# A third home for one chunk's inputs, weights converted by pairs, and attention pieces placed by hand in the first unit

## The chip, the cores and the metric

One Trainium2 chip, one of its cores. The metric is the time of one execution on the device in microseconds (us); lower is better. Engines are named as the profile names them: PE is TensorE (PEld its weight loads), DVE is VectorE, ACT is ScalarE, POOL is GpSimd, SP is SyncE, which here only issues DMAs.

## The reference

```python
# 1: linear attention with decay, B=4, H=8, S=768, D=48
for t in range(S):
    state = alpha[:, :, t, :, None] * state + np.einsum('bhd,bhe->bhde', k[:, :, t], v[:, :, t])
    y[:, :, t] = np.einsum('bhd,bhde->bhe', q[:, :, t], state)
# 2: x = y as [3072 tokens, 384]; squared-ReLU layer, d_ff = 2048
h = np.maximum(x @ w_in, 0.0)
x = h * h @ w_out
# 3: 8 experts, each token to one of them by its sorted gate logits, 384 tokens an expert
logits = x @ w_gate
...
    h = np.maximum(x[mask] @ w1[e], 0.0)
    out[mask] = h @ w2[e]
```

The weights `w_in` and `w_out` come into the kernel as 64-bit floats and are made into 32-bit ones on the chip.

## The kernel before

The tokens are cut into 24 chunks of 128 (six to a batch entry), and three chunks make a unit of 384 tokens: 8 units. Attention (`attn`) is done by chunks, and the squared-ReLU layer by units: for each of 16 blocks `f` of 128 hidden features, `moe_a` multiplies the unit's tokens into a PSUM tile `ph` (line 388, 9 matmuls), `moe_ev` squares the ReLU and splits it into a high and a low part `hl` (for unit 0: three ACT passes at lines 393, 397 and 401, then a DVE subtraction at line 404), and `moe_b`, two steps later, multiplies `hl` by the block of `w_out` (line 416, 9 matmuls). Each product is made of three, with both factors split in two, so that it has nearly the precision of 32 bits.

A step is one value of `g` (unit and block). The first 18 steps, `first_step`, are the first unit and the first two blocks of the second one. They are under a hand-written order: on PE, DVE, ACT and POOL instructions stand as the code emits them, and a queue that waits holds all that is behind it. What stands ahead of the first step is listed in `ORDER`: the letters name pieces of chunks 0 to 3 (`p` and `a` two scans on DVE, `q` the scaled `kt` and `qt`, `s` the scores, `n` a transposed `kn`, `o` the result), `C` and `S` the two parts of a weight conversion, `w` a dummy matmul.

What each step of the first unit holds besides `moe_a`, `moe_ev` and `moe_b`:

- Conversion. Two blocks of weights a step (one of `w_in`, one of `w_out`), each in `narrow`: three integer passes on DVE over 128x384 words (lines 348, 350, 352), from a raw tile `rawi` or `rawo` into `wf` or `wfo`. In the next step, ACT rounds the block into `wbuf` (line 355), and POOL subtracts for the low part (line 356). A raw tile is loaded again as soon as its third pass is over; `rawi` has three homes, `rawo` two.
- The gate columns (`gate_w`): the expert gate is folded into `w_out`, so each block of `w_out` is transposed on PE (line 450), copied by ACT (line 452), multiplied by the gate weights into eight spare columns of `ph` (line 455), and split into `wbuf` by ACT (line 457) and DVE (line 459).
- Attention for the next units: `attend` gives a number of pieces for the step, by `PACE`, and they are emitted behind `moe_b`. Chunks 3 to 6 are done in this way within the 18 steps.

Two PSUM banks hold `ph`. The matmuls at line 388 of step `g` can start only when the last reader of the bank of step `g - 2` is done; that is line 459, which stands behind line 404 on DVE.

The inputs of a chunk (alpha, k, q; 677 KB) go to one of two tiles `akq0`, `akq1`. Chunk 2 therefore waits until chunk 0 has let go of its tile.

## Time and profile before

| What | Value |
|---|---|
| Time, median of 3 runs | 868.7 us (868.61 to 869.08) |
| The profiled execution: its time, and its span | 867.91 us, 865.7 us |
| PE busy | 813.1 us, 94% of the span |
| DVE busy | 498.1 us, 58% |
| ACT, POOL busy | 337.6 us, 366.3 us |
| Mean granted TensorE clock | 0.975 of full speed |

The span runs from the first to the last instruction on the core; 2.2 us of the profiled execution's time lie around it, and that execution is 0.8 us faster than the median. The shares are means over stages with different limits. The change touches the stage from 0 to about 145 us; behind it come the other units, the routing and the experts.

### The profile page before, as it was taken

The page shows a single profiled execution, that of the slowest core. Times are in us where ns is not written, and L with a number is a line of the kernel's source. Part 1 is how long each engine was busy: PE and PEld are TensorE (multiplying, and loading weights), DVE is VectorE, ACT ScalarE, POOL GpSimd, SP SyncE. Part 2 cuts the span into 40 slices and gives each one's busy share as a digit, 9 for nine tenths or more (in the row PEclk, how much of TensorE's full clock was granted, in tenths as well). Part 3 has the DMA queues.
Part 4 walks back from the last instruction along what each step waited for, and adds up shares of the span by engine and source line. Part 5 has one row for each costly group of instructions (what it writes and reads, how often), then busy time and mean ns, then how long its engine had stood idle before and what let it go on. Part 6 is the DMA issues. An engine that isn't in the chain of part 4 may idle for free.

```text
span 865.7 us, 14472 instructions
## 1 busy us (share of the span) xinstructions
PE 813.1 (94%) x5752; PEld 755.0 (87%) x5752; DVE 498.1 (58%) x1149; ACT 337.6 (39%) x615; POOL 366.3 (42%) x350
## 2 busy tenths in 40 slices
PE   7699999999999999999999999986999999999994
PEld 6588898999999999999999998875887888889993
DVE  7999884444444434435434213476876877876730
ACT  2265464233234233233233334213435536536620
POOL 2456562343342343343242344125457567572511
PEclk9899899999999999999999999996999999999997
DMA  8545322112112112112100000031432522513500
GB/s 257 158 160 188 125 76 79 42 49 69 43 49 70 42 49 70 42 49 74 64 23 28 1 23 13 15 143 49 173 129 74 201 97 105 192 69 141 199 31 30
DMA packets 21626, 75.54 MB, mean 87 GB/s; under 512 B 3137, under 2 KB 10178, under 8 KB 19634
## 3 DMA queue, kind: packets, MB, share of 16 engines
q0 software_dynamic: 5520, 34.61, 10.9%
q1 hardware_dynamic: 11682, 25.72, 9.4%
q10 hardware_dynamic: 4352, 14.24, 5.5%
q8 instruction: 46, 0.75, 0.4%
q14 instruction: 26, 0.21, 0.1%
HBM read 63.84 MB, written 9.54 MB: 85 GB/s over the span
## 4 chain that ended last, share of the span: by engine, by line
PE 76%; DVE 11%; ACT 5%; DMA 3%; issue 2%; POOL 0%; SPq 0%; POOLq 0%; DVEq 0%; ACTq 0%
PE ph L388 22%; PE p L416 20%; PE ph L988 9%; PE py L1006 7%; ACT wbuf L951 3%; PE psc L252 3%; DVE wbuf L953 3%; PE py L273 2%; PE p L671 2%; PE py L270 2%; DMA akq<-in_akq_dram 2%; DMA w1s<-in_moe_w_dram,wi 2%; PE pn L292 1%; DVE hl L997 1%; PE pu L303 1%
## 5 line engine op out<-in xcount | busy, mean ns | idle before, releaser
L388 PE MATMUL ph<-xT,wbuf 128*128 128x384 f32 x1152 | 228.3, 342 | 7.2 <-DVE wbuf L459 5.0
L388 PEld LDWEIGHTS ph<-xT,wbuf 128*128 128x128 f32 x1152 | 206.1, 190 | 10.9 <-DVE wbuf L459 6.0
L416 PE MATMUL p<-wbuf,hl 128*128 128x392 f32 (+1 forms) x1008 | 204.1, 346 | 0.0
L400 DVE SCALAR_TENSOR_TENSOR s<-ph,s 128x384 f32<-128x384 f32 x112 | 62.3, 557 | 223.4 <-ACT s L393 222.9
L416 PEld LDWEIGHTS p<-wbuf,hl 128*128 128x128 f32 x1008 | 177.8, 189 | 4.0 <-issue 3.0
L404 POOL TENSOR_TENSOR hl<-s,hl 128x384 fp32r<-128x384 f32 x96 | 97.6, 1017 | 184.3 <-ACT hl L401 176.3
L393 ACT ACTIVATE s<-ph 128x384 f32<-128x384 f32 x128 | 63.1, 493 | 175.7 <-PE ph L388 138.9
L1006 PE MATMUL py<-wbuf,hl 128*128 128x384 f32 x576 | 125.3, 348 | 0.0
L988 PE MATMUL ph<-xt,wbuf 128*128 128x384 f32 x576 | 118.4, 349 | 1.4 <-DVE xt L963 0.9
L988 PEld LDWEIGHTS ph<-xt,wbuf 128*128 128x128 f32 x576 | 100.2, 190 | 4.7 <-DVE xt L963 2.3
L1006 PEld LDWEIGHTS py<-wbuf,hl 128*128 128x128 f32 x576 | 99.0, 188 | 0.7
L401 ACT ACTIVATE hl<-s 128x384 fp32r<-128x384 f32 x96 | 50.4, 525 | 73.6 <-DVE s L400 73.6
L996 ACT ACTIVATE hl<-ph 128x384 fp32r<-128x384 f32 x64 | 31.8, 497 | 114.1 <-PE ph L988 110.4
L997 DVE SCALAR_TENSOR_TENSOR hl<-ph,hl 128x384 fp32r<-128x384 f32 x64 | 35.5, 555 | 35.0 <-ACT hl L996 35.0
L951 ACT ACTIVATE wbuf<-w1s 128x1024 fp32r<-128x1024 f32 x24 | 52.2, 2221 | 2.5 <-DMA w1s<-in_moe_w_dram,wi 2.5
L1014 POOL DMA_INDIRECT out_dram<-o,idx x24 | 28.6, 1193 | 50.9 <-ACT o L1011 19.8
L953 POOL TENSOR_TENSOR wbuf<-w2s,wbuf 128x768 fp32r<-128x768 f32 x24 | 43.5, 1837 | 6.0 <-ACT wbuf L951 6.0
L245 POOL TENSOR_TENSOR sad<-state,ae 48x192 f32<-48x192 f32 x40 | 25.1, 628 | 37.7 <-DVE state L309 28.6
L759 POOL DMA_INDIRECT xg<-x2d,row x24 | 23.0, 957 | 38.9 <-DVE idx L815 14.9
L356 POOL TENSOR_TENSOR wbuf<-wf,wbuf 128x384 fp32r<-128x384 f32 x16 | 21.1, 1322 | 37.9 <-ACT wbuf L355 37.9
L225 DVE TENSOR_TENSOR_SCAN suf<-akq,fresh 112x516 f32<-112x516 f32 x24 | 31.8, 1325 | 4.9 <-DMA akq<-in_akq_dram 4.4
L953 POOL TENSOR_TENSOR wbuf<-w1s,wbuf 128x1024 fp32r<-128x1024 f32 x11 | 32.9, 3014 | 3.0 <-ACT wbuf L951 2.9
(211 smaller groups left out, 1091.0 us busy)
## 6 DMA issues: line engine op xcount, KB each, us to landing
akq<-in_akq_dram ACTq DMA_DIRECT2D x16, 677.2 KB, 4.5
rawi<-in_moe_w_in_dram SPq DMA_DIRECT2D x16, 384.0 KB, 3.3
rawo<-in_moe_w_out_dram SPq DMA_DIRECT2D x16, 384.0 KB, 3.9
akq<-in_akq_dram SPq DMA_DIRECT2D x7, 677.2 KB, 5.6
x2d<-xo SPq DMA_DIRECT2D x24, 192.0 KB, 2.0
v<-in_v_dram ACTq DMA_DIRECT2D x16, 192.0 KB, 2.4
v<-in_v_dram SPq DMA_DIRECT2D x8, 192.0 KB, 6.9
xf<-xf SPq DMA_DIRECT2D x16, 72.0 KB, 2.6
```

Of the source, the lines that this page charges most:

```text
L225: dve.tensor_tensor_scan(back(one(P)), back(one(al)), back(one(fresh)), 1.0, op0=OP.mult, op1=OP.add)
L388: pe.matmul(ph[:, :UT], win[:, wi, kt, fs], XT[u][:, xi, kt, :], start=n == 0, stop=n == 3 * KT - 1)
L393: act.activation(s, ph[:, :UT], AF.Relu)
L400: dve.scalar_tensor_tensor(s, ph[:, :UT], 0.0, s, op0=OP.max, op1=OP.mult)
L401: act.activation(hl[:, 0], s, AF.Copy)
L404: (dve if u == 0 or (u, f) == (NU - 1, FT - 1) else pool).tensor_tensor(hl[:, 1], s, hl[:, 0].bitcast(F32), op=OP.subtract)
L416: pe.matmul(PY[u][t][:, :w], hl[:, si, t * C:(t + 1) * C], wout[:, wi, f, :w], start=f == 0 and n == 0, stop=f == FT - 1 and n == 2)
L951: act.activation(dst[:, 0], src, AF.Copy)
L953: (dve if "d" in e else pool).tensor_tensor(dst[:, 1], src, dst[:, 0].bitcast(F32), op=OP.subtract)
L988: pe.matmul(ph[:, :CAP], wa[:, wi, kt, j, :], xt[:, xi, kt, :], start=n == 0, stop=n == 3 * KT - 1)
L997: dve.scalar_tensor_tensor(hl[:, 1], ph[:, :CAP], 0.0, hl[:, 0].bitcast(F32), op0=OP.max, op1=OP.subtract)
L1006: pe.matmul(PX[k, i][:, :DM], hl[:, hi_, i * 128:(i + 1) * 128], wb[:, wi, j, :], start=j == 0 and n == 0, stop=j == FT2 - 1 and n == 2)
```

## The change

Four things, all ahead of the end of the first unit:

1. Chunk 2's inputs go to a third tile, `extra`, which is the first home of the new raw tile, and are loaded at the start. In `ORDER` one conversion moves from ahead of chunk 2's `s` to behind it, and chunk 3 is gone from it.
2. Weights are loaded and converted by pairs: `convert` makes three DVE passes over 128x768 words in place of six over 128x384. ACT and POOL still work block by block. A raw pair has two homes.
3. Chunks 3 to 6 start at the steps `BEGIN`; each of their pieces has a place in the six steps from there, so that what one engine makes in a step another uses in the next. In the step, the subtraction of `moe_ev` now stands ahead of the conversion on DVE, and the transposes of `gate_w` behind `moe_b` on PE.
4. The gate columns are gathered in `wgate` by ACT, and split once, after the unit, for all 16 blocks.

```diff
-ORDER = ("... 1q 2p 1s 1n 2a 2q 1o w C 2s S C 2n w w 2o x w w w w "
-         "w w w w w w w w S 3p 3a C S 3q L C w").split()
-SEQ = [(0, 0), (0, 1), (0, 2), (1, 0)] + [x for f in range(1, FT) for x in ((0, f + 2), (1, f)) if x[1] < FT]
-PACE = 3.75, 0.9375
+ORDER = ("... 1q 2p 1s 1n 2a 2q 1o w 2s C S C L 2n w w 2o x w w w w "
+         "w w w w w w w w S C L w").split()
+PAIRS = [((0, 0), (0, 1)), ((0, 2), (1, 0))] + [((0, f + 2), (1, f)) for f in range(1, FT - 2)] + [((1, 14), (1, 15))]
+BEGIN = 1, 5, 8, 12
...
+    def raw_tile():
+        return cp_.tile([128, 4 * DM + 3 * NP], I32, name="raw", bufs=2)
+    extra = raw_tile()[0:112].bitcast(F32).rearrange("p (i a t) -> p i a t", i=3, a=NP)
+    NAT = lambda ch: extra if ch == 2 else nat[ch % 2]
...
     load(1)
     load_v(0)
+    load(2)
     load_v(1)
+    load_v(2)
...
+        if ch >= CPU:
+            kn2 = turn()
+            yield "s"
+            mask(0, NP)
+            yield "m"
+            pu = None if last else update()
+            yield "u"
+            if not last:
+                keep(pu)
+            result(0, NP)
+            yield "o"
+            return
...
+    def convert(n, halves=(0, 1)):
+        if 0 in halves:
+            wf[n] = cp_.tile([128, 2, DM], F32, name="wf", bufs=WF)
+        h = slice(halves[0], halves[-1] + 1)
+        dst = wf[n][:, h].bitcast(I32)
+        w = raw[n][:, h].rearrange("p h (n two) -> p h n two", two=2)
+        lo, hi = w[:, :, :, 0], w[:, :, :, 1]
         dve.tensor_scalar(dst, hi, 3, 0x3FFFFFFF, op0=OP.logical_shift_left, op1=OP.bitwise_and)
         yield
         dve.scalar_tensor_tensor(dst, lo, 29, dst, op0=OP.logical_shift_right, op1=OP.bitwise_or)
         yield
         dve.scalar_tensor_tensor(dst, hi, -(1 << 30), dst, op0=OP.bitwise_and, op1=OP.bitwise_or)
+        if 1 in halves and n + 2 < len(PAIRS):
+            due.append(n + 2)
+        yield
+        for i in halves:
+            second, f = PAIRS[n][i]
+            t = wf[n][:, i]
...
+            act.activation(to[0], x, AF.Copy)
+            pool.tensor_tensor(to[1], x, to[0].bitcast(F32), op=OP.subtract)
+            if second:
+                tasks.append(gate_w(f, x))
+        yield
...
         yield
-        act.activation(wout[:, 0, f, DM:], ph[:, DM:W], AF.Copy)
-        yield
-        dve.tensor_tensor(wout[:, 1, f, DM:], ph[:, DM:W], wout[:, 0, f, DM:].bitcast(F32), op=OP.subtract)
+        act.activation(wgate[:, f], ph[:, DM:W], AF.Copy)
         yield
...
     def first_step(g):
         u, f = steps[g]
+        for i, at in enumerate(BEGIN):
+            if g - at in (4, 5):
+                go(early[i])
...
         while begun:
             go(begun.pop(0))
+        for e in old:
+            go(e)
+        start_conv()
+        if g >= 2:
+            moe_b(0, g - 2)
         for t in tasks:
             next(t)
-        start_conv(2 if g < FT - 3 else 1)
-        for e in old:
-            go(e)
-        for t in hi:
-            next(t)
-        if g >= 2:
-            moe_b(0, g - 2)
-        for _ in range(attend(g)):
-            piece()
+        for i, at in enumerate(BEGIN):
+            if 0 <= g - at <= 4:
+                go(early[i])
...
     go(before.pop(), 2)
+    act.activation(wout[:, 0, :, DM:], wgate, AF.Copy)
+    pool.tensor_tensor(wout[:, 1, :, DM:], wgate, wout[:, 0, :, DM:].bitcast(F32), op=OP.subtract)
```

DVE's queue in a step of the middle of the unit, before: the two conversions (`wf` and `wfo` in turn), the subtraction `hl` of the step before, the gate columns, and one piece of a chunk's attention (`suf` is the first scan).

```order
L348 TENSOR_SCALAR wf<-rawi 128x384
L348 TENSOR_SCALAR wfo<-rawo 128x384
L350 SCALAR_TENSOR_TENSOR wf<-rawi,wf 128x384
L350 SCALAR_TENSOR_TENSOR wfo<-rawo,wfo 128x384
L352 SCALAR_TENSOR_TENSOR wf<-rawi,wf 128x384
L352 SCALAR_TENSOR_TENSOR wfo<-rawo,wfo 128x384
L404 TENSOR_TENSOR hl<-ph,hl 128x384
L459 TENSOR_TENSOR wbuf_65<-ph,wbuf_65 128x8
L225 SCALAR_TENSOR_TENSOR suf<-akq_75,fresh 112x516
```

The same queue with the change, two steps (1 and 2) with the first scan of chunk 3 and, a step later, its second one (`A`).

```order
L382 TENSOR_SCALAR wf<-raw 128x768
L384 SCALAR_TENSOR_TENSOR wf<-raw,wf 128x768
L386 SCALAR_TENSOR_TENSOR wf<-raw,wf 128x768
L233 SCALAR_TENSOR_TENSOR suf<-akq_76,fresh 112x516
L431 TENSOR_TENSOR hl<-ph,hl 128x384
L382 TENSOR_SCALAR wf<-raw 128x768
L384 SCALAR_TENSOR_TENSOR wf<-raw,wf 128x768
L386 SCALAR_TENSOR_TENSOR wf<-raw,wf 128x768
L235 RECIPROCAL whole<-suf 112x4
L237 SCALAR_TENSOR_TENSOR A<-akq_76,whole 112x515
```

Six passes have become three of twice the width, the gate columns are gone, and the subtraction `hl` (now line 431) stands ahead of its step's conversion.

PE's queue before, around the step that ends with a chunk's scores (`psc`), and the next one:

```order
L388 MATMUL ph<-xT,wbuf_64 128x384 x9
L455 MATMUL ph<-wg,gx 128x8 x3
L450 MATMUL pt<-ident,wfo 128x128 x3
L416 MATMUL p_553<-wbuf_65,hl 128x384 x3
L416 MATMUL p_554<-wbuf_65,hl 128x384 x3
L416 MATMUL p_555<-wbuf_65,hl 128x384 x3
L252 MATMUL psc<-qt,kt 128x128 x8
L292 MATMUL pn<-ident,kt 128x112 x4
L388 MATMUL ph<-xT,wbuf_64 128x384 x9
```

The same place with the change (step 8, the scores of chunk 4, and the start of step 9):

```order
L415 MATMUL ph<-xT,wbuf_64 128x384 x9
L483 MATMUL ph<-wg,gx 128x8 x3
L443 MATMUL p_464<-wbuf_65,hl 128x384 x3
L443 MATMUL p_465<-wbuf_65,hl 128x384 x3
L443 MATMUL p_466<-wbuf_65,hl 128x384 x3
L478 MATMUL pt<-ident,wf 128x128 x3
L260 MATMUL psc<-qt,kt 128x128 x8
L296 MATMUL pn<-ident,kt 128x112 x4
L415 MATMUL ph<-xT,wbuf_64 128x384 x9
```

The three transposes `pt` have moved behind the nine matmuls of `moe_b`.

DVE's queue at the end of the unit with the change: `kt` and `qt` of chunk 6, then pieces of chunks 7 and 8 (which no hand-written place holds), with the last two subtractions `hl` (steps 14 and 15) between them.

```order
L241 TENSOR_TENSOR kt<-akq_75,suf 112x512
L242 TENSOR_TENSOR qt<-akq_75,A 112x512
L233 SCALAR_TENSOR_TENSOR suf<-akq_76,fresh 112x516
L235 RECIPROCAL whole<-suf 112x4
L237 SCALAR_TENSOR_TENSOR A<-akq_76,whole 112x515
L431 TENSOR_TENSOR hl<-ph,hl 128x384
L242 TENSOR_TENSOR qt<-akq_76,A 112x512
L266 TENSOR_TENSOR Pt<-psc,causal 128x512 x2
L241 TENSOR_TENSOR kt<-akq_76,suf 112x512
L233 SCALAR_TENSOR_TENSOR suf<-akq_75,fresh 112x516
L235 RECIPROCAL whole<-suf 112x4
L237 SCALAR_TENSOR_TENSOR A<-akq_75,whole 112x515
```

Before, chunk 8's scan stood behind the last subtraction; now it stands ahead of it.

## Rows read from the trace of the kernel before

**Rows 1.** Busy time by stretch: window and length, then PE, PEld, DVE, ACT, POOL, clock.

```profile
31.00:44.00 13.00, 6.23 (x42) 5.36 (x41) 12.79 (x18) 2.04 (x4) 6.55 (x7) 0.72 0.46 134
31.00:121.00 90.00, 78.21 (x548) 74.18 (x546) 83.34 (x146) 46.46 (x108) 53.09 (x41) 0.91 0.45 143
160.00:540.00 380.00, 380.00 (x2664) 362.66 (x2659) 152.33 (x259) 132.97 (x272) 136.43 (x159) 1.00 0.14 44
```

**Rows 2.** Waits of PE, then DVE, from 31 and 26 to 121: us, times, longest.

```profile
PE pt L450 <- DVE wfo L352: 6.8, 1, 6.8
PE ph L388 <- DVE wbuf L459: 5.0, 3, 2.0
...
DVE Pt L258 <- PE psc L252: 3.1, 1, 3.1
DVE hl L404 <- ACT hl L401: 2.0, 2, 1.1
DVE state L309 <- PE pu L303: 1.7, 2, 0.9
```

**Rows 3.** Timeline of DVE around chunk 2: start, duration, what, idle time before.

```profile
17.06 1.23 DVE L225 TENSOR_TENSOR_SCAN suf<-akq,fresh 112x516 f32<-112x516 f32 x1 [2.60 <-DMA akq<-in_akq_dram]
...
19.39 0.17 DVE L227 RECIPROCAL whole<-suf 112x4 f32<-112x4 f32 x1
...
20.80 0.66 DVE L233 TENSOR_TENSOR kt<-akq,suf 112x512 f32<-112x512 f32 x1
...
22.75 0.43 DVE L348 TENSOR_SCALAR wf<-rawi 128x384 int32<-128x384 int32 x1
...
24.59 1.42 DVE L258 TENSOR_TENSOR Pt<-psc,causal 128x128 f32<-128x128 f32 x4
```

**Rows 4.** Timeline of DVE, conversions: first alone, then two in turn.

```profile
35.36 0.33 DVE L348 TENSOR_SCALAR wf<-rawi 128x384 int32<-128x384 int32 x1
...
36.79 0.68 DVE L233 TENSOR_TENSOR kt<-akq,suf 112x512 f32<-112x512 f32 x1
...
69.52 0.34 DVE L348 TENSOR_SCALAR wf<-rawi 128x384 int32<-128x384 int32 x1
69.79 0.35 DVE L348 TENSOR_SCALAR wfo<-rawo 128x384 int32<-128x384 int32 x1
...
71.94 0.54 DVE L404 TENSOR_TENSOR hl<-ph,hl 128x384 fp32r<-128x384 f32 x1
```

**Rows 5.** Timeline of DVE and POOL around 61 us.

```profile
60.94 0.15 DVE L459 TENSOR_TENSOR wbuf<-ph,wbuf 128x8 fp32r<-128x8 f32 x1
61.01 0.16 DVE L227 RECIPROCAL whole<-suf 112x4 f32<-112x4 f32 x1
...
62.98 1.28 DVE L348 TENSOR_SCALAR wfo<-rawo 128x384 int32<-128x384 int32 x1
...
60.72 1.00 POOL L356 TENSOR_TENSOR wbuf<-wf,wbuf 128x384 fp32r<-128x384 f32 x1 [1.52 <-ACT wbuf L355]
61.68 2.36 POOL L356 TENSOR_TENSOR wbuf<-wfo,wbuf 128x384 fp32r<-128x384 f32 x1
```

**Rows 6.** Timeline of PE: the first steps, and the last of the unit.

```profile
31.66 1.84 PE L388 MATMUL ph<-xT,wbuf 128*128 128x384 f32 x9
...
43.80 3.23 PE L388 MATMUL ph<-xT,wbuf 128*128 128x384 f32 x9
...
117.37 1.75 PE L388 MATMUL ph<-xT,wbuf 128*128 128x384 f32 x9
...
121.52 1.75 PE L388 MATMUL ph<-xT,wbuf 128*128 128x384 f32 x9
...
131.63 1.84 PE L388 MATMUL ph<-xT,wbuf 128*128 128x384 f32 x9
```

**Rows 7.** DMA issues: queue, kind, count, KB each, median us from issue to landing.

```profile
rawo<-in_moe_w_out_dram SPq DMA_DIRECT2D x16, 384.0 KB, 3.9
akq<-in_akq_dram SPq DMA_DIRECT2D x7, 677.2 KB, 5.6
```

More of the change, by code (lines that the diff above doesn't have):

```diff
@@ L217, in attn @@
         vn = vnat[ch % 3].rearrange("p (h d) -> p h d", h=H)
-        al, kn, qn = (nat[ch % 2][:, i] for i in range(3))
+        al, kn, qn = (NAT(ch)[:, i] for i in range(3))
         v4 = lambda t: t.rearrange("p (a t) -> p a t", a=NP)
@@ L280, in result, with turn, update, keep @@
                     sp.dma_start(x[o + 48:o + 64, :KT, :], x[o:o + 48, KT, :])
+        def turn():
+            if last:
+                return
+            pn = bank(next(tag), "pn")
+            for p in range(NP):
+                pe.transpose(pn[:, p * 128:p * 128 + 112], kt[:, p], ident[0:112, 0:112])
+            kn2 = ap_.tile([128, NP, 2, D], F32, name="kn2", bufs=1)
+            n4 = v4(pn).rearrange("p k (j d) -> p k j d", j=2)
+            act.activation(kn2, n4[:, :, :, :D], AF.Copy)
+            return kn2
+        def update():
+            pu = bank(next(tag), "pu")
+            for p in range(NP):
+                for j in range(2):
+                    o = 64 * j
+                    pe.matmul(pu[o:o + D, p * 64:p * 64 + D], kn2[:, p, j], vn[:, 2 * p + j],
+                              start=True, stop=True)
+            return pu
+        def keep(pu):
+            for j in range(2):
+                o = 64 * j
+                src = v4(pu[o:o + D, 0:256])[:, :, 0:D]
+                if c:
+                    dve.tensor_tensor(state[o:o + D], src, sa[o:o + D, :, o:o + D], op=OP.add)
+                else:
+                    (act.copy if ch == 0 else dve.tensor_copy)(state[o:o + D], src)
+        if ch >= CPU:
[9 more added lines that the diff above has]
+            yield "o"
+            return
         if late:
@@ L288, in attn @@
         yield "s"
[L289 to L314 removed]
+        kn2 = turn()
+        yield "n"
+        if not late:
+            keep(update())
         result(0, NP - late)
         if late:
[L317 removed]
+            keep(update())
         yield "o"
@@ L333, in attention @@
     def attention():
-        for ch in range(CPU, NCH):
+        for ch in range(CPU + len(BEGIN), NCH):
             for n in attn(ch):
@@ L431, in moe_kernel @@
     tasks = []
+    wgate = cp_.tile([128, FT, E], F32, name="wgate")
     def by_gate(x):
@@ L479, in moe_kernel @@
     warm = bank("h", "warm")
-    convs = [(conv_out if w else conv_in)(f) for w, f in SEQ]
-    convs = iter(convs)
+    ends = 0, len(PAIRS) - 1
+    convs = iter([convert(n, h) for n in range(len(PAIRS)) for h in (((0,), (1,)) if n in ends else ((0, 1),))])
     begun = []
@@ L518, in moe_kernel @@
         else:
-            done += what[0] == "3" and what[1] != "s"
             go(gens[int(what[0])])
         if what == "0q":
-            load_in(0)
-            load(2)
-            load_v(2)
-            load_out(0)
-            load_in(1)
+            load_pair(0)
+            load_pair(1)
             sp.dma_start(wg.rearrange("p k e -> p (k e)"), w_gate)
@@ L566, in attend @@
         n = 0
-        while done < (PACE[0] + PACE[1] * g if g < FT else (g + LEAD) * RATE):
+        while done < (g + LEAD) * RATE:
             done += 1
@@ L572, in piece @@
     def piece():
-        if next(att, None) == "s":
+        if next(att, None) in ("s", "u"):
             next(att)
@@ L613, in moe_kernel @@
     before, before_gate = [], []
+    early = [attn(CPU + i) for i in range(len(BEGIN))]
     for g in range(FT + 2):
```

97 lines of the change are left out of this document (26 added, 71 removed).

## The prediction

> **What bounds the kernel now.** The page first: PE is busy 94% of the span, so most of the kernel is PE's, and from 160 to 540 us it has no idle time at all [rows 1]. The exception that this change touches is the first unit. From 31 to 121 us PE is busy 78.2 of 90 us, so 11.8 us are lost, and DVE is busy 83.3 of 90 [rows 1]. The waits say the same: PE stood 6.8 us for line 352 (the conversion) and 5.0 us for line 459, the last thing that a step does on DVE [rows 2]. The first two groups of line 388 are 12.1 us apart, the later ones 4.15 us where PE waits for nothing [rows 6]. So in this stage DVE sets the pace. DVE itself waited little: 3.1, 2.0 and 1.7 us are the entries that matter from 26 us on [rows 2].
>
> Part of DVE's busy time is waiting, too. The POOL subtraction of line 356 takes 1.00 us when it has its way [rows 5]. The one at 61.68 lasts until 64.04, and the DVE pass that starts at 62.98, 0.34 us long when undisturbed [rows 4], ends at 64.26: it began only when POOL was done [rows 5]. Conversions on DVE and subtractions on POOL take turns, and a step has about 2.4 us of the one and 2.0 us of the other. This makes the stage a matter of DVE and POOL together, and not one of hand-overs alone.
>
> Since PE is saturated behind the unit [rows 1], a microsecond won here should come through whole, and I work the sum at a marker: the start of line 388's group of step 15, now 121.52 [rows 6], and then look at what follows it.
>
> **The change part by part.**
>
> *Chunk 2's own home, and `ORDER`.* Its first scan waited 2.60 us for its inputs, and started at 17.06, so DVE was free at 14.46 [rows 3]. With the load at the start, the scan can begin then. A conversion stood between 22.75 and 24.59, ahead of the mask of chunk 2 [rows 3]; it now stands behind. The mask of chunk 2 ended at 24.59 + 1.42 = 26.0. It would end at 26.0 - 2.6 - 1.8 = 21.6; the scores of the chunk before still have to be ready in between, for which I give 0.5: 22.1. Gain 3.9 at this point of DVE's queue. Bounds: if the inputs land late (they share the queue with others, and 677 KB took 5.6 us in the median, [rows 7]), up to all of the 2.6 is lost, so 1.3 to 4.4.
>
> *From there to the marker, DVE has the same work.* Before, behind the mask: 3 conversions alone and 13 pairs, then 2 alone; with the change 3 alone (two at the start, one at step 13) and 14 pairs. The conversion moved behind the mask, and two others moved past the marker's last subtraction (one became half of a pair). So conversions: one alone less and one pair more less one alone, that is 2 x 1.43 - 2.42 = 0.4 less, with 1.43 for one alone (35.36 to 36.79) and 2.42 for a pair (69.52 to 71.94) [rows 4]. Against it, chunk 6 starts so much earlier that its second scan, 1.4 us with the reciprocal (19.39 to 20.80, [rows 3]), falls ahead of the marker. Chunks 3 to 6 are moved within the unit, not taken away. The difference is 1.0 more. It comes back behind the marker, where that scan no longer stands, so over both places it is nothing.
>
> *Pairs.* Two conversions in turn start 0.27 us apart in the first pass and need 2.42 us [rows 4]. One alone needs 1.43, more than half of that, because each pass waits for the one before it. A pair made by three passes is three dependent passes: 1.43 plus the second half's elements, 2.42 - 1.43 = 0.99 if they cost what they do now. That is 2.42 again, and I take 0. Lower bound: if part of a pass is a price by the instruction, three are saved. A pass of 0.27 and one of 0.47 ((2.42 - 2 x 0.27) / 4) give a fixed part of 0.07 if the short one goes at twice the rate, so 0.21 a step and 2.9 us in 14 steps. Upper bound: 0.1 a step more, 1.4 us.
> [...]
>
> *Line 459 is gone.* It is 0.07 us from its start to that of the next (60.94 to 61.01, [rows 5]), 13 times: 0.9 less. Its place is taken by one ACT copy and one POOL subtraction over 128x128 behind the unit, each under 1.0 us (the 384-word POOL subtraction, [rows 5]); they have over 3 us (two groups of nine matmuls) before `moe_b` of the second unit wants them.
>
> *The hand-overs.* The 3.1 us that DVE waited for scores (`psc`) go, since the mask now stands a step behind the matmuls. Of the 1.7 for `state`, 0.9 go for the same reason; the rest is ahead of the unit. The 2.0 for `hl` I leave: the subtraction now stands ahead of the conversion, and so may wait for ACT. What hides this is that DVE is late: the 14 steps from 43.80 to 121.52 took 5.55 us each [rows 6], and with more of attention inside them I count 5.7, against 4.15 for PE. With that cover gone it would be up to 1.1 us a step, the longest such wait [rows 2]. New: the third pair's load can be issued only when the second's home is free, and I give 0.9 for one wait on it at step 1. So 3.1 + 0.9 - 0.9 = 3.1 less.
>
> *POOL* has the same 1.00 us subtractions. They find three gaps between DVE's passes and not six, and more masks beside which to run; from 0 to 0.1 us a subtraction either way, 30 of them: 3 us to both sides, and I take 0.
>
> *Behind the marker.* Before, the matmuls of step 17 start 10.1 us after the marker (131.63, [rows 6]). Now two scans each of chunks 7 and 8 stand ahead of the subtractions that release PE's banks. Those of chunk 8 also wait for inputs whose load ACT issues behind a copy of the step's transposes, at about 4.15 + 0.5 us. With 5.6 for the landing [rows 7], 1.2 and 1.4 for the scans and 0.7 for `qt`, I get some 13.5 us in place of 10.1. On the other side chunk 6's last matmuls then stand ahead of that group and not behind it, and DVE is free for the second unit's first blocks, where it was late before. I take 0 for the end, with 1 better to 3 worse as bounds.
>
> **The sum.** At the marker 3.9 + 3.1 + 0.9 - 1.0 (the scan) = 6.9 less, and the 1.0 comes back behind it: 7.9, say 8 less in all. 867.91 - 8 = 859.9 for the profiled execution, whose span is 865.7 with 2.2 around it. The median is 0.8 above that execution, so 860.7.
>
> **The rivals.**
>
> *PE becomes the bound.* If one hand-over a step frees PE of all waits, the 11.8 us [rows 2] go and the start 3.4 us earlier comes on top: 868.7 - 15.2 = 853.5. For it speaks that PE's waits are exactly on the two lines that move. Against it: DVE and POOL still have to do in turn what fills 83 of the 90 us [rows 1].
>
> *Fewer passes are cheaper.* The fixed part of 0.07 us, three times in 14 steps, makes 2.9 less: 857.8. Against it are the passes in turn, which show no such price left to save. [...]
>
> *Only the head.* If the hand-overs change nothing, because what DVE doesn't wait for it pays to POOL, 3.9 remain, less what late inputs take: 864.8, or 867.4 at the worst bound. The change would then not do what it says. For it: DVE's idle time was only 6.7 us of 90 [rows 1], so little is there to win.
>
> *The loads come late (slower).* Raw pairs have two homes where `rawi` had three. From the end of one conversion to the start of the next but one are two steps less one conversion with POOL's turns in it, 2 x 5.7 - 4 = 7.4 us. A landing is 3.9 us, that of a chunk's inputs 5.6 [rows 7]. A pair behind such inputs may need 9.5, their sum, and lose 2.1; few steps have such a load. The point from which it decides is a mean landing of 8.0 us (0.57 x 14 = 8, all that is won). At 8.5 us the loss is 1.1 x 14 = 15, and the kernel is at 876, slower. Against it: `rawo` has two homes already, and no wait for it stands among DVE's waits.
>
> **How the numbers follow.** Chances: my sum (856 to 863.5) 0.5, with the cheaper passes at 0.12 inside its faster half; PE the bound (852 to 856) 0.2; only the head (863.5 to 867) 0.17; no change that counts 0.06; late loads or a worse end, slower, 0.07. About 0.2% (1.7 us) is what a measurement of this kernel can tell from no change. The time is that of the likeliest, 860.7; the range 853.5 to 866.5 leaves out the far ends of the two neighbours, the slower cases and little else. Faster 0.87, same 0.06, slower 0.07.
>
> **What the new profile would show.** Chunk 2's first scan at about 14.5. The first group of the `ph` matmuls near 28 and the second near 32.5, where it was at 43.8. Then steps of about 5.7 us with DVE busy nearly all the time, and PE waiting for the subtraction `hl`. A pair's three passes at 2.4 us from start to end where POOL is idle. The marker near 114.5. I am wrong if PE has no waits from step 4 on (then it is PE's stage), or if the raw loads show among DVE's waits.

## The result, and the profile after

The changed kernel takes 859.84 us (median of 4 runs, 859.5 to 861.29), the kernel before in the same comparison 868.75 (median of 4, 868.61 to 869.08): a ratio of 0.9900, 95% interval 0.9883 to 0.9917, or 8.9 us less. The forecast was 860.7. The profiled execution took 859.59 with a span of 857.3, so 8.4 of span against before. The sum was right. Most of its terms were not, and what follows is about those.

In the changed kernel line 415 is `moe_a` (388 before), 443 `moe_b` (416), 431 the subtraction `hl` (404), 478 the transposes `pt` (450), 382, 384 and 386 the conversion's passes (348, 350, 352), 399 and 400 its ACT and POOL parts (355, 356), and 531 the dummy matmuls. The stretches of [rows 1], after:

```profile
31.00:121.00 90.00, 83.18 (x616) 79.06 (x616) 88.13 (x101) 50.82 (x117) 55.56 (x46) 0.99 0.47 154
160.00:540.00 380.00, 380.00 (x2660) 362.18 (x2659) 152.88 (x260) 134.47 (x276) 138.11 (x166) 1.00 0.14 43
```

In 31 to 121 us PE is busy 5.0 us more than before, DVE 4.8 more, and the granted clock is 0.99 where it was 0.91. DVE still sets the pace: it is busy in 88 of 90 us. But from 83.7 us to the marker PE waits for nothing either, so that late in the unit the two are level. The waits that answer to [rows 2], of PE from 28 and of DVE from 22 to 121 us (total, times, longest):

```profile
PE ph L415 <- DVE hl L431: 4.5, 4, 2.2
PE pt L478 <- DVE wf L386: 1.1, 3, 0.5
...
DVE state L316 <- PE pu L307: 2.7, 1, 2.7
```

PE's 6.8 us for the first conversions are 1.1; for `ph` it still waits 4.5, now on `hl`. DVE's waits for scores and for ACT's `hl` are gone, and there is none for a raw tile. PE's timeline, with the steps that answer to [rows 6] and the head ahead of them:

```profile
25.23 1.65 PE L278 MATMUL py<-qt,sad 112*128 112x128 f32 x6 [1.90 <-ACT kn L299]
...
28.90 4.41 PE L531 MATMUL warm<-ones 128*128 128x128 f32 x26
33.07 1.83 PE L415 MATMUL ph<-xT,wbuf 128*128 128x384 f32 x9
...
110.75 1.83 PE L415 MATMUL ph<-xT,wbuf 128*128 128x384 f32 x9
...
118.97 2.19 PE L415 MATMUL ph<-xT,wbuf 128*128 128x384 f32 x9 [2.19 <-DVE hl L431]
...
127.48 0.80 PE L415 MATMUL ph<-xT,wbuf 128*128 128x384 f32 x3
```

The first group comes 1.4 us later than before and not 3.7 earlier; the second is at 35.50 (43.80 before); the marker (step 15) at 110.75, 10.8 earlier and not 6.9. So 8.3 of the 10.8 us are there at the second group already; DVE no longer does chunk 3's scans and products ahead of it. The 14 steps from there take 5.38 us each where they took 5.55, though they now hold those pieces; the forecast had 5.7. From the marker to step 17 it takes 16.7 us where it took 10.1. The transposes for the second unit (line 465) begin at 132.73, against 141.44: of the 10.8 us, 8.7 are left there. Once PE works without a gap, 7.3 are left (the second unit's group of line 415 at 140.69, of line 388 at 148.00 before). The span shows 8.4.

A part of what is lost behind the marker is the granted clock. This is PE in the first profile of the changed kernel (clock: third number from the end), and under it in a second one, a_again of the next section:

```profile
120.00:124.00 4.00, 4.00 (x17) 4.00 (x16) 3.84 (x6) 0.98 (x2) 0.19 (x1) 0.54 0.34 103
```

```profile
120.00:124.00 4.00, 3.10 (x42) 2.59 (x41) 3.81 (x6) 1.77 (x4) 0.19 (x1) 1.00 0.64 177
```

With the clock at 1.00 there, step 17 comes 14.9 us behind the marker (109.43 and 124.37).

The head on DVE, which answers to [rows 3], and under it ACT:

```profile
13.96 1.53 DVE L233 TENSOR_TENSOR_SCAN suf<-raw,fresh 112x516 f32<-112x516 f32 x1
...
21.37 1.42 DVE L266 TENSOR_TENSOR Pt<-psc,causal 128x128 f32<-128x128 f32 x4 [0.81 <-PE psc L260]
...
29.09 0.74 DVE L316 TENSOR_TENSOR state<-pu,sad 48x192 f32<-48x192 f32 x2 [2.71 <-PE pu L307]
```

```profile
24.27 0.52 ACT L399 ACTIVATE wbuf<-wf 128x384 fp32r<-128x384 f32 x1 [1.62 <-DVE wf L386]
24.70 0.47 ACT L299 ACTIVATE kn<-pn 128x384 f32<-128x384 f32 x1
```

The scan started 3.1 us earlier and the mask ended at 22.79 instead of 26.01. But ACT rounded the first weight block (line 399) ahead of the copy of `kn`, and had to wait for DVE's conversion first. PE stood 1.90 us for that copy, and from 24 to 32 us its granted clock was 0.59 and 0.56, where it was 1.00 before. So the head's gain did not reach the first group. The clock has the larger part in this: in a_again PE stood the same 1.90 us for the copy, the clock was 1.00 from 24 to 32 us, and the first group came at 30.19, 2.9 us sooner than here.

**DVE from chunk 2's mask to the marker.** This is the stretch that the sum was about, and DVE does the same attention and the conversions of 31 blocks in it, in both kernels. DVE's row for it, before and after (length, busy time, instructions, clock):

```profile
26.01:121.52 95.51, 87.30 (x152) 0.91 0.45 144
```

```profile
22.79:110.75 87.96, 82.97 (x98) 0.96 0.51 167
```

It became 7.55 us shorter: 3.2 of idle time (8.21 to 4.99) and 4.3 of busy time. The groups show where the busy time went. First the kernel before, then after (count, busy us, mean ns, idle ahead):

```profile
L225 DVE TENSOR_TENSOR_SCAN suf<-akq,fresh 112x516 f32<-112x516 f32 x4 | 7.2, 1795 | 0.0
L229 DVE TENSOR_TENSOR_SCAN A<-akq,whole 112x515 f32<-112x515 f32 x4 | 5.9, 1470 | 0.1
L234 DVE TENSOR_TENSOR qt<-akq,A 112x512 f32<-112x512 f32 x3 | 3.0, 988 | 0.0
L233 DVE TENSOR_TENSOR kt<-akq,suf 112x512 f32<-112x512 f32 x3 | 2.8, 948 | 0.0
```

```profile
L233 DVE TENSOR_TENSOR_SCAN suf<-akq,fresh 112x516 f32<-112x516 f32 x4 | 5.2, 1304 | 0.0
L237 DVE TENSOR_TENSOR_SCAN A<-akq,whole 112x515 f32<-112x515 f32 x4 | 5.2, 1290 | 0.1
L241 DVE TENSOR_TENSOR kt<-akq,suf 112x512 f32<-112x512 f32 x3 | 2.1, 687 | 0.0
L242 DVE TENSOR_TENSOR qt<-akq,A 112x512 f32<-112x512 f32 x3 | 2.1, 685 | 0.0
```

The same 14 instructions take 14.6 us instead of 18.9: 4.3 less. What held them up before is seen on two timelines, DVE and POOL of the kernel before:

```profile
66.59 1.48 DVE L233 TENSOR_TENSOR kt<-akq,suf 112x512 f32<-112x512 f32 x1
68.00 1.60 DVE L234 TENSOR_TENSOR qt<-akq,A 112x512 f32<-112x512 f32 x1
...
66.51 1.02 POOL L356 TENSOR_TENSOR wbuf<-wf,wbuf 128x384 fp32r<-128x384 f32 x1 [2.21 <-ACT wbuf L355]
67.48 1.57 POOL L356 TENSOR_TENSOR wbuf<-wfo,wbuf 128x384 fp32r<-128x384 f32 x1
```

`kt` and `qt` need 0.69 us each when alone; here each met a POOL subtraction and ended 0.54 and 0.55 us behind its end. In the changed kernel the same pair stands behind the conversion, past POOL's two:

```profile
51.20 1.77 DVE L384 SCALAR_TENSOR_TENSOR wf<-raw,wf 128x768 int32<-128x768 int32 x1
...
53.88 0.69 DVE L241 TENSOR_TENSOR kt<-akq,suf 112x512 f32<-112x512 f32 x1
54.48 0.69 DVE L242 TENSOR_TENSOR qt<-akq,A 112x512 f32<-112x512 f32 x1
...
49.18 2.98 POOL L400 TENSOR_TENSOR wbuf<-wf,wbuf 128x384 fp32r<-128x384 f32 x2 [2.44 <-ACT wbuf L399]
```

POOL now meets mainly the conversion's second pass (1.77 us here and 1.59 in the mean of its 14 from the mask to the marker, 0.96 alone), and the piece of attention goes free. In these rows DVE's instruction waits out POOL's: before, `kt` started 0.08 us behind a subtraction and took 1.48 us, 0.79 more than alone. Why they take turns is not shown.

### The profile page after: what moved, and what is told of

The parts are those of the page before. It is cut to its first block, busy times and chain, and to the rows that moved or that the text cites. A ratio compares the mean times of both kernels' runs of the same rounds, so it can differ in the third digit from the quotient of the medians.

```text
span 857.3 us, 14404 instructions
## 1 busy us (share of the span) xinstructions
PE 812.6 (95%) x5752; PEld 755.4 (88%) x5752; DVE 493.4 (58%) x1091; ACT 338.0 (39%) x616; POOL 361.7 (42%) x351
## 4 chain that ended last, share of the span: by engine, by line
PE 72%; DVE 15%; ACT 5%; issue 4%; DMA 2%; POOL 0%; POOLq 0%; SPq 0%; DVEq 0%; ACTq 0%
PE ph L415 20%; PE p L443 19%; PE ph L1011 9%; PE py L1029 7%; ACT wbuf L974 3%; DVE wf L384 3%; DVE wbuf L976 3%; PE psc L260 3%; PE py L281 3%; PE p L694 2%; PE py L278 2%; DMA w1s<-in_moe_w_dram,wi 2%; DVE wf L382 1%; PE pu L307 1%; PE pn L296 1%
## 5 line engine op out<-in xcount | busy, mean ns | idle before, releaser
L415 PEld LDWEIGHTS ph<-xT,wbuf 128*128 128x128 f32 x1152 | 203.8, 188 | 7.5 <-DVE hl L431 5.4
L400 POOL TENSOR_TENSOR wbuf<-wf,wbuf 128x384 fp32r<-128x384 f32 x32 | 42.1, 1334 | 33.3 <-ACT wbuf L399 33.3
L782 POOL DMA_INDIRECT xg<-x2d,row x24 | 22.9, 954 | 38.8 <-DVE idx L838 14.9
L260 PE MATMUL psc<-qt,kt 48*128 48x128 f32 x384 | 28.8, 291 | 3.4 <-DVE qt L242 3.4
```

What stands on the lines that cost most here:

```text
L260: pe.matmul(psc[j][:, p * 128:(p + 1) * 128], kt[o:o + D, p], qt[o:o + D, p], start=True, stop=True)
L400: pool.tensor_tensor(to[1], x, to[0].bitcast(F32), op=OP.subtract)
L415: pe.matmul(ph[:, :UT], win[:, wi, kt, fs], XT[u][:, xi, kt, :], start=n == 0, stop=n == 3 * KT - 1)
```

## The experiments

Theory: DVE and POOL in turns set the pace of the first unit, the head's gain was lost to the copy of `kn`, and the tail's to scans that stand ahead of a subtraction. Rivals: hand-overs or PE set it, and one part of the change carries the gain. A profile is one execution, and two of the same kernel differ (see b_again and a_again). The table holds, for each run, the ratio to the kernel before on the same chip (0.0010 is 0.9 us), and of its profiled execution the end of chunk 2's mask, the marker, and DVE's busy and idle time between them.

| Kernel | Ratio (95%) | Mask end | Marker | DVE busy | Idle |
|---|---|---|---|---|---|
| before | 1 | 26.01 | 121.52 | 87.30 | 8.21 |
| b_again: before | 1.0009 (0.9975 to 1.0043) | 25.34 | 120.55 | 89.22 | 5.99 |
| after | 0.9900 (0.9883 to 0.9917) | 22.79 | 110.75 | 82.97 | 4.99 |
| a_again: after | 0.9900 (0.9866 to 0.9934) | 22.81 | 109.43 | 82.97 | 3.65 |
| e1: `kn` first | 0.9864 (0.9831 to 0.9897) | 21.73 | 107.58 | 82.60 | 3.25 |
| e2: two in turn | 0.9891 (0.9860 to 0.9922) | 26.63 | 115.87 | 85.95 | 3.29 |
| e3: POOL twice | 1.0048 (1.0026 to 1.0071) | 22.89 | 119.01 | 92.53 | 3.59 |
| e4: scans held | 0.9875 (0.9835 to 0.9914) | 21.91 | 109.51 | 82.95 | 4.65 |
| e5: mask in the same step | 0.9884 (0.9861 to 0.9907) | 22.81 | 109.21 | 82.72 | 3.68 |
| e6: `hl` behind | 0.9920 (0.9895 to 0.9945) | 26.01 | 119.46 | 86.99 | 6.46 |
| e7: no home | 0.9907 (0.9874 to 0.9941) | 25.41 | 113.35 | 82.92 | 5.02 |
| e8: e1 and e4 | 0.9856 (0.9826 to 0.9886) | 24.15 | 109.45 | 82.86 | 2.44 |
| e9: before, `hl` ahead | 1.0009 (0.9982 to 1.0036) | 26.12 | 122.16 | 87.34 | 8.70 |
| e10: gate each step | 0.9891 (0.9860 to 0.9921) | 22.61 | 110.23 | 82.96 | 4.66 |

**e1: the copy of `kn` first.**

```diff
-... 2s C S C L 2n w w 2o x ...
+... 2s C 2n S C L w w 2o x ...
```

> The one edit: in the list of head entries, the copy of chunk 2's normalised keys (2n) goes ahead of the conversion and its ACT pass (S C L). Theory (the 3.2 us that DVE won in the head were lost because this copy stood behind an ACT pass that waited for DVE until 24.24): the 1.9 us that PE waited for the copy at 25.23 go to under 0.5, the first group of the ph matmuls comes at 28.5 to 30.5 instead of 33.07, the marker (the start of that group in step 15) at 107 to 109 instead of 110.75, and the time falls by 2 to 3.5 us, to about 857. If the granted clock of 24 to 32 us (0.59 and 0.56) followed from that wait, it rises too. Rival (the steps are bound by DVE and POOL behind it, and these make up or lose the same whatever the head does): first group earlier, marker and time as they were, 859.8 within 0.7.

Measured: 859.16 us (857.52 to 860.42), ratio 0.9864, 3.1 us below that of the changed kernel. In its profile ACT copies `kn` at 21.94, PE waits 0.18 us for it, and the first group starts at 27.43:

```profile
22.49 0.94 PE L278 MATMUL py<-qt,sad 112*128 112x128 f32 x6 [0.18 <-ACT kn L299]
...
27.43 1.99 PE L415 MATMUL ph<-xT,wbuf 128*128 128x384 f32 x9
31.97 0.91 PE L478 MATMUL pt<-ident,wf 128*128 128x128 f32 x3 [2.55 <-DVE wf L386]
```

That the wait comes from the copy's place in ACT's queue is shown: it goes when the copy moves. The 26 dummy matmuls ahead of that group take 3.17 us, as they do in a_again at a clock of 1.00, and not 4.41 as above, and the marker comes 3.2 earlier (1.9 against a_again). But 1.1 of this stands at chunk 2's mask, ahead of the copy, and so is not the edit's. PE then waits 2.55 us for the second conversion, so DVE takes part of the gain. The size in the time is not settled: the intervals overlap.

**e2: two conversions in turn.**

```diff
-    convs = iter([convert(n, h) for n in range(len(PAIRS)) for h in (((0,), (1,)) if n in ends else ((0, 1),))])
+    convs = iter([convert(n, h) for n in range(len(PAIRS)) for h in ((0,), (1,))])
...
-        start_conv()
+        start_conv(2 if g < FT - 3 else 1)
...
```

> The one edit: where a step converts a pair of blocks by three passes of 128x768, it converts the same two blocks as two conversions of 128x384 whose passes alternate, six passes; all else, the loads by pairs and the order of hand-overs too, stays. Theory of the prediction (passes in turn hide the latency, so the pair costs the same 2.4 us): 859.8 within 1.4, marker at 110.75 within 1.4. Rival (a fixed price for each pass, 0.07 us each, three passes in each of 14 steps): 2.9 us slower, 862.7. A second rival (six gaps between passes instead of three, in which the POOL subtractions get their turn): up to 0.1 us a subtraction, as much as 3 us either way.

Measured: 861.77 us (858.7 to 864.61), ratio 0.9891, no difference that counts. The rival of a fixed price (2.9 us) is not borne out. The theory's latency is a pass's wait for the one before it: in the trace behind [rows 4] the passes of one conversion alone start 0.36 and 0.60 us apart (at 35.36, 35.72 and 36.32), those in turn 0.27 and 0.47, and two take 2.42 us and not twice 1.43. What touches `wf` in the stretch, after and in e2 (busy PE, PEld, DVE, ACT, POOL):

```profile
22.79:110.75 87.96, 7.58 (x45) 7.03 (x45) 56.28 (x52) 17.78 (x31) 40.96 (x31) 0.96 0.51 167
```

```profile
26.63:115.87 89.24, 7.55 (x45) 7.10 (x45) 55.34 (x94) 18.21 (x31) 41.25 (x31) 0.98 0.49 158
```

94 short passes cost DVE 0.9 us less than 52 that are mostly long. The pieces of attention cost 3.7 more instead (18.3 in place of 14.6, `qt` 1.50 us in the mean in place of 0.69): POOL met them again. The profiled execution is the slowest of its six, so this is one picture, and its mask came late ahead of all these passes: it waited 3.19 us for `psc`.

**e3: POOL twice.**

```diff
+                pool.tensor_tensor(to[1], x, to[0].bitcast(F32), op=OP.subtract)
                 tasks.append(gate_w(f, x))
```

> The one edit: POOL computes the subtraction of each w_out block twice over, into the same tile; the output is the same. Theory (in the first unit DVE's passes and POOL's subtractions take turns, and the two together set the pace of a step): some 30 more subtractions of 1.0 us fall into DVE's time, so a step of 5.38 us becomes 6.0 to 6.4 us and the time rises by 9 to 15 us, to about 869 to 875. Rival (the hand-overs between PE, ACT and DVE set the pace and POOL works beside them; POOL is busy 55.6 of the 90 us from 31 to 121): 0 to 2 us more, 860 to 862.

Measured: 874.23 us (871.69 to 876.77), ratio 1.0048, 12.9 us above the changed kernel's. The theory is shown and its rival refuted: 14 more subtractions fall between mask and marker (one for each pair, not the 30 that the expectation counted), and DVE's busy time there grows by 9.6 us, though DVE got no instruction more. The conversions alone go from 56.3 to 64.2.

**e4: the scans held.**

```diff
+        if g >= FT - 1:
+            next(att)
+            done += 1
         for i, w in enumerate(SPLIT):
...
```

> The one edit: the first three pieces of chunk 7's attention are placed at the ends of steps 15, 16 and 17 instead of wherever the even spreading puts them (its scans now stand ahead of the last subtractions of the unit). Theory (of the 10.8 us that the marker came earlier, 2 to 3 were given back behind it, because the scans of chunk 7 delay the subtraction that PE waits 2.19 us for): that wait goes, the group of step 17 comes 2 to 3 us sooner than 127.48, and the time falls by 1 to 3 us, to 857 to 859. Rival (those scans have to be done anyway before the second unit, and what is won at step 17 is lost ahead of its blocks): 859.8 within 0.7, with the second unit's first block at 133.8 as it was.

Measured: 858.69 us (855.55 to 863.4), ratio 0.9875. The wait of 2.19 us at step 16 is gone; what is left there is 0.63 for POOL's `xT`, and the transposes for the second unit start at 128.23 (132.73 after, 129.24 in a_again). That the scans' place made the wait is shown. But behind those transposes PE stands 2.10 us for POOL, which splits the gathered gate columns (line 645 here, 642 in the changed kernel):

```profile
131.65 1.87 PE L443 MATMUL p<-wbuf,hl 128*128 128x392 f32 x9 [2.10 <-POOL wbuf L645]
```

The second unit's group that a_again has at 137.03 comes at 136.81. So the rival holds in this pair of profiles: what is won at step 17 is lost ahead of the second unit's blocks. The time, 2.2 us less by the ratio, is inside the intervals.

**a_again and b_again: no edit.**

> The changed kernel once more, with no edit, as the baseline of the three runs beside it. Every theory expects 859.8 us within 2; a spread over its executions like the 8 us seen over those of the kernel before in the last comparison would go with the mean granted clock of each execution.

> The kernel before once more, with no edit, for a second profile. Theory A (what the changed kernel gained on DVE between chunk 2's mask and the marker is in the order of the work, so it is the same in each execution): DVE busy for 87 to 88 us in that stretch again, 4 more than the 83.0 that the changed kernel shows, and the psc wait of 3.1 us at 102.80 again. Theory B (a part of it was the granted clock, which fell to half at 40 to 48 and at 92 to 100 us in the first profile, and made PE late): where the second dip is missing, the psc wait of 3.1 us is gone and the marker comes 2 to 3 us sooner than 121.52.

Measured: 861.09 (855.63 to 864.99) and 869.78 us (868.4 to 877.55). In a_again the first group comes at 30.19 and not at 33.07: PE waits 1.90 for `kn` here too, but the clock is 1.00 from 24 to 32. DVE's busy time to the marker is 82.97 in both profiles of the changed kernel, 87.3 and 89.2 in the two of the kernel before. That difference belongs to the order of the work, as theory A has it (its range was 87 to 88). The `psc` wait does not. In the first profile of the kernel before, the stretch from 92 to 96 us (clock: third number from the end) and then DVE:

```profile
92.00:96.00 4.00, 4.00 (x17) 4.00 (x17) 4.00 (x8) 1.88 (x6) 1.16 (x2) 0.50 0.28 92
```

```profile
102.80 1.29 DVE L258 TENSOR_TENSOR Pt<-psc,causal 128x512 f32<-128x512 f32 x2 [3.12 <-PE psc L252]
```

In b_again the clock was 1.00 in the same stretch, and DVE never waited for `psc`:

```profile
92.00:96.00 4.00, 2.87 (x20) 2.54 (x19) 4.00 (x9) 2.78 (x7) 1.78 (x3) 1.00 0.33 96
```

So the 3.1 us were PE, late behind a stretch at a clock of 0.50. Theory B is right on the wait; the marker came 1.0 earlier, not 2 to 3. Behind the marker the second profile of the changed kernel gives back less than the first: the second unit's group of line 415 is at 137.03, 10.0 us ahead of b_again's (147.03), after 11.1 at the marker.

**e5: the mask in the same step.**

```diff
             kn2 = turn()
-            yield "s"
             mask(0, NP)
+            yield "s"
             yield "m"
```

> The one edit: in the unit's chunks the mask stands right behind the scores of its own step again, and the step that it had moves on by one. Theory (the 3.1 us that DVE waited for psc went because the mask stands a step behind its scores): DVE waits for psc again at lines 260 and 266, about 3 us in four chunks, and the marker and the time come 2 to 3 us later, 862 to 863. Rival (in the changed kernel DVE's gain is in the passes that POOL holds up less, and a wait for psc only takes the place of such a hold-up): 859.8 within 1.

Measured: 859.55 us (859.23 to 860.69), ratio 0.9884. DVE does not wait for `psc` once between 22 and 122 us, although the mask stands behind its own scores again. The theory is refuted: the hand-over of a mask a step later is worth nothing here.

**e6: `hl` behind the conversion.**

```diff
+        start_conv()
         for e in old:
             go(e)
-        start_conv()
```

> The one edit: the conversion of a step stands ahead of the subtraction hl on DVE again, as in the kernel before, in place of behind it. Theory of the prediction (DVE is late in every step, so the order of the two changes only who waits): PE's wait for hl grows from 4.5 us, as each subtraction comes 2.4 us later, but DVE's own work to the marker is the same; the marker moves by less than 1.5 us, 859.8 within 1.5. Rival (PE's hand-over sets the pace: matmuls ahead of hl, hl, matmuls behind it): up to 1 us a step, 12 us, 865 to 872.

Measured: 862.11 us (861.67 to 868.36), ratio 0.9920, 1.7 us above the changed kernel. The rival of 1 us a step is refuted. The theory's 1.5 us for the time is neither shown nor refuted. The profiled execution is the slowest of the six, by 6 us over four of them: its clock was 0.58 and 0.57 from 16 to 24 us, its mask waited 3.52 us for `psc`, and PE waited 4.13 us for `hl` at step 2. In it the marker came 8.7 us later, and DVE's busy time is 87.0 again, against the theory. A part of these 4.0 us is work that stood behind the marker (two conversion passes and one `kt`), and a part is pieces that are held up again:

```profile
L237 DVE TENSOR_TENSOR_SCAN A<-akq,whole 112x515 f32<-112x515 f32 x4 | 6.3, 1584 | 0.1
...
L241 DVE TENSOR_TENSOR kt<-akq,suf 112x512 f32<-112x512 f32 x4 | 5.1, 1278 | 0.0
```

**e7: no home of its own for chunk 2.**

```diff
-    NAT = lambda ch: extra if ch == 2 else nat[ch % 2]
+    NAT = lambda ch: nat[ch % 2]
...
-    load(2)
...
             load_pair(0)
+            load(2)
             load_pair(1)
```

> The changed kernel with one edit undone: chunk 2's inputs go to chunk 0's tile again, and are loaded when that is free. Theory of the prediction (the home is worth 3.9 us at chunk 2's mask, and all of it comes through): 3 to 4 us slower, 863 to 865. Theory after the traces (the head's gain was lost to the key copy's place on ACT and to the granted clock, since the first group of ph came at 33.07 and 30.19 in two profiles, and at 31.66 before): chunk 2's mask ends 2 to 3 us later, and the marker and the time move by 0 to 2.6 us, 860 to 863.

Measured: 864.23 us (857.06 to 868.27), ratio 0.9907. Its scan waits 3.64 us for its inputs and starts at 17.73; the mask ends at 25.41, 2.6 later than after, and the marker is 2.6 later than after (3.9 than a_again), with the stretch between and DVE's busy time unchanged. So in these profiles the home is worth 2.6 us at the mask and keeps them to the marker. By the ratio it is 0.6 us, with an interval that holds both.

**e8: e1 and e4 together.**

> Two edits: chunk 2's key copy ahead of the conversion's ACT pass in the head, and chunk 7's first three pieces at the ends of steps 15 to 17. Theory (both are time that the change left on the table, at different places): the second unit's first block at 125 to 126.5 instead of 132.73 and the time 4 to 6 us below the changed kernel run beside it, 854 to 856. Rival (what is won ahead of 130 us is lost again where the third stage begins, at 580 us, as in the profiled execution with the first edit alone): the same as the changed kernel within 1.5.

Measured: 857.57 us (854.63 to 862.73), ratio 0.9856, beside 861.09 for the changed kernel on the same chip. By the ratios that is 3.8 us less, with intervals that just overlap, and a little short of the 4 to 6 that the theory has. It is the lowest median of all, but not clear of e1 or e4. The second unit's blocks did not come at 125 to 126.5: after a first matmul at 128.42 PE waits 2.10 us for POOL's split here too, and goes on at 131.59. The profiled execution is the slowest of the six, so it does not show where the others gain.

**e9: the kernel before, with `hl` ahead of the conversion.**

```diff
-        start_conv(2 if g < FT - 3 else 1)
         for e in old:
             go(e)
         for t in hi:
             next(t)
+        start_conv(2 if g < FT - 3 else 1)
```

> The kernel before with one part of the change alone: in a step, the subtraction hl and the gate columns' subtraction stand ahead of the conversion on DVE. Theory (with the conversion ahead, POOL's subtractions meet the scans and the scaling of k and q; the run that put it back in the changed kernel had 87.0 us of DVE busy to the marker instead of 83.0): DVE busy to the marker 83 to 85 instead of 87.3, PE's waits for lines 352 and 459 shorter, 2 to 5 us faster than the kernel before, 864 to 867. Rival (the passes that POOL holds up are others, since the conversions still are six passes and the pieces of attention stand elsewhere): the same as the kernel before within 1.7.

Measured: 871.68 us (867.67 to 879.13), ratio 1.0009. The theory is refuted and the rival holds: DVE is busy 87.34 us, as before. The first scans got shorter (`suf` 5.7 instead of 7.2) and the second ones longer (`A` 1.86 us in the mean instead of 1.47), the conversions took 63.2 instead of 60.4 by the groups' sums, and DVE waited 5.6 us for ACT's `hl`. PE's wait for line 459 fell to 1.1, and that for line 352 rose to 10.8.

**e10: the gate columns in each step.**

```diff
-        act.activation(wgate[:, f], ph[:, DM:W], AF.Copy)
+        act.activation(wout[:, 0, f, DM:], ph[:, DM:W], AF.Copy)
         yield
+        dve.tensor_tensor(wout[:, 1, f, DM:], ph[:, DM:W], wout[:, 0, f, DM:].bitcast(F32), op=OP.subtract)
+        yield
...
+        for t in hi:
+            next(t)
         start_conv()
...
```

> The changed kernel with one edit undone: the gate columns of each block are split in the step again, by ACT into the weights and by the DVE subtraction of 128x8 right behind hl, instead of once behind the unit. Theory of the prediction (0.07 us of DVE each, 13 times, 0.9 in all, and the last reader of PE's bank comes that much later): DVE busy to the marker 83.9 instead of 83.0, marker and time 0.9 later, 860.5 to 862. Rival (PE's bank waits for the reader behind hl, so the wait of 5.0 us that PE had for it in the kernel before comes back in part): 2 to 4 us, 862 to 864.

Measured: 863.29 us (861.25 to 865.25) beside 872.91 for the kernel before on that chip, ratio 0.9891. With 13 subtractions more (2.0 us by their group), DVE's busy time is 82.96, as without them; the conversions behind them take 55.7 us by the groups' sums instead of 56.6, so these were held up that much less. DVE's time speaks against the theory; the ratio cannot, as its interval holds 0.9 us more. The rival's 2 to 4 us lie just outside the interval, and PE waits about as long for the new last reader (4.7 us) as it did for `hl` (4.5).

## Why the prediction was right, and where it was wrong

**The forecast of the time** held (859.84 against 860.7), by terms whose errors cancelled, and that is luck: 10.8 us at the marker where it said 6.9, and 3.5 given back by the second unit's groups where it said 1.0 more. A second pair of profiles (a_again and b_again) has 11.1 and 1.1, so the errors are there too.

**The head, 3.9.** Measured 3.2 at the mask in the first profile, with 2.6 of it from the home (e7), both inside the bounds. Its next step, the first group near 28 us, failed: the prediction followed DVE's queue alone and did not see that the copy of `kn` stands behind an ACT pass which waits for that DVE. e1 moves the copy and gets 27.43. The rest of the miss is the clock (30.19 in a_again).

**DVE's idle time, 3.1.** Measured 3.2 (2.3 between the second profiles), but not by the terms named. What went in both pairs is the wait for ACT's `hl` (2.0 and 1.7), which the prediction left in. The 0.9 for `state` inside the unit went, but the wait for it ahead of the unit grew from 0.8 to 2.7 in the first pair. The 0.9 for a raw tile is missing from the changed kernel's profiles; e1 has one such wait, of 0.71 us. The wait for `psc` stood behind a stretch at a clock of 0.50 and is missing from a second profile of the kernel before, where that was 1.00; e5 shows that the mask's place does not matter here. A single wait ("3.1, 1, 3.1" in [rows 2]) was taken for a property of the order.

**Line 459, 0.9.** Nothing on DVE (e10): what the small pass took, the conversion behind it was held up less. Its replacement behind the unit, which the prediction took as free, is free in the two profiles of the changed kernel; PE waits 2.10 us for it in e4 and e8.

**The second scan of chunk 6, 1.0 the other way.** Nothing: it started ahead of the marker before, too. The row was there to be read, 1 us ahead of 121.52:

```profile
120.47 1.41 DVE L229 TENSOR_TENSOR_SCAN A<-akq,whole 112x515 f32<-112x515 f32 x1
```

**Pairs, 0.** Right for the passes themselves: 0.9 more of DVE by e2, within the bounds of 2.9 less and 1.4 more. A pair's passes where POOL is idle start 0.59, 1.00 and 0.87 us apart, 2.46 in all (2.42 in turn, [rows 4]):

```profile
33.12 0.96 DVE L384 SCALAR_TENSOR_TENSOR wf<-raw,wf 128x768 int32<-128x768 int32 x1
34.12 0.96 DVE L386 SCALAR_TENSOR_TENSOR wf<-raw,wf 128x768 int32<-128x768 int32 x1
34.99 0.55 DVE L382 TENSOR_SCALAR wf<-raw 128x768 int32<-128x768 int32 x1
35.58 0.96 DVE L384 SCALAR_TENSOR_TENSOR wf<-raw,wf 128x768 int32<-128x768 int32 x1
```

No run shows a price by the instruction: passes that alternate between two tiles start 0.27 us apart in [rows 4], three dependent ones took no less time than the six, and the 94 short passes of e2 took 55.34 us where the 52 took 56.28. The bound of 2.9 took the short pass at twice the rate of a long one, and the traces agree with that much: 384 words more cost the short one 0.22 us (0.33 and 0.55) and the long one 0.40 (0.56 and 0.96).

**POOL, 0 with 3 to both sides.** This is the term that was mis-sized: 4.3 us less, outside its bound (5.9 between the second profiles), in the 14 scans and products of attention, which no longer meet POOL's subtractions. The prediction had the mechanism in its first part ([rows 5]) and then priced it by the subtraction; the price fell on the DVE pass that stood there, 0.79 us on `kt` before (1.48 and 0.69) and 0.63 in the mean on a conversion's second pass after (1.59 and 0.96). No single edit was shown to carry it. With pairs undone DVE is busy 85.95, with the order undone 86.99, with the order alone 87.34; the first two come from the slowest executions of their kernels, with masks that waited 3.19 and 3.52 us for `psc`, and two profiles of the kernel before differ by 1.9 with no edit at all. Undone one at a time, pairs, mask, order, home and gate cost -0.8, -1.4, 1.7, 0.6 and -0.8 us by the ratios, each uncertain by some 3 us, and nothing near 8.9 together. What was not undone by itself is the place by hand of the pieces of chunks 3 to 6, chunk 3's going from `ORDER` with it, and the transposes behind `moe_b` on PE. That the places carry the rest is argued from the rows above, and not shown; the transposes are an untested rival. That POOL's work costs DVE's time is shown (9.6 us for 14 more subtractions in e3); which part of the change takes it away is open.

**Behind the marker, 0.** At the transposes 2.1 us worse, at the second unit's groups 3.5, beyond the bound of 3; in the second pair 0.1 better and 1.1 worse, inside it. The group of step 17 came 16.7 us behind the marker, not 13.5. Of these 3.2 us, 1.8 go with the clock (14.9 in a_again, where it did not fall). In both, chunk 7's scans met POOL (below they take 2.04 and 2.16 us, where chunk 8's take 1.23 and 1.29) and held up the subtraction that PE waited 2.2 us for:

```profile
114.01 2.04 DVE L233 TENSOR_TENSOR_SCAN suf<-akq,fresh 112x516 f32<-112x516 f32 x1
...
116.30 2.16 DVE L237 TENSOR_TENSOR_SCAN A<-akq,whole 112x515 f32<-112x515 f32 x1
118.39 0.53 DVE L431 TENSOR_TENSOR hl<-ph,hl 128x384 fp32r<-128x384 f32 x1
```

**The signs.** Steps of 5.7 us from a second group at 32.5 would put the marker at 112.3 and not at 114.5, so these did not fit each other. Measured are 35.50, 5.38 and 110.75.

**The rivals.** PE is not the bound of the whole unit: from 28 us to the marker it waits 4.5 us (3.9 in a_again), all for DVE. But the sign for it, no waits from step 4 on, came true from step 10 to step 15: PE came near to being the bound, and ahead of the marker little more than those waits is left to win from DVE. The loads are not late: raw blocks land in 3.1 and 3.8 us in the median, far from 8.0. Only the head: refuted by the stretch that became 7.55 us shorter.

## What to carry to other kernels

Where instructions of two engines take turns, as DVE's and POOL's did here, an instruction's price depends on what the other engine does at that moment (`kt` took 0.69 us alone and 1.48 behind a subtraction): look at how far the same instruction's mean lies above its duration alone, and place the pieces by that, not by their count. A single wait of 3 us is not yet a property of the order: see what the clock was just ahead of it (0.50 ahead of the 3.12 us for `psc`, and 1.00 where that wait was missing). And follow a moved piece through every engine's queue up to the next hand-over, ACT's too: behind an ACT pass that waited 1.62 us, the copy of `kn` cost PE 1.90 us, and 0.18 ahead of it.
